# Windowed attention and a gated FFN: transposes of x, q and k moved from TensorE to the DMA engines

## The chip, the cores and the metric

One core of a Trainium2 chip runs the whole kernel. The time is device microseconds of one execution; a median over several executions is quoted.

## The reference

```python
# q, k, v: (4 batches, 8 heads, 768, 64) f32
keep = (pos_k < 4) | ((pos_q - pos_k >= 0) & (pos_q - pos_k < 128))   # 4 sink keys and a window of 128
a = softmax(where(keep, q @ k.T / sqrt(64), -1e9));  attn = a @ v
x = attn.transpose(0, 2, 1, 3).reshape(3072, 512)
xn = x / rms(x) * rms_g
out = (silu(xn @ w_gate) * (xn @ w_val)) @ w_out      # 512 -> 1536 -> 512
```

## The kernel before

The 3072 rows are 24 blocks of 128 rows (six to a batch), and four blocks make a group for the FFN: groups 0 to 5. All matmuls are bf16. TensorE's order is written by hand; a list of attention units ("slots", four to a block) is woven between the FFN's parts. The orders of the other engines come from a scheduler.

Three operands have to be turned so that their columns lie on the partitions: q and k of each block (for the scores) and the normalised x (for the gate and value matmuls). TensorE does it, 128x128 at a time into PSUM, and ScalarE copies the result to SBUF:

```python
MANUAL = {mybir.EngineType.PE}

def unit_t(g):                                   # q and k of block g: 8 transposes, one copy
    b, t = divmod(g, NT)
    if t == 0:
        QKT[b] = qkt.tile([P, 2, HP, S], BF16, name="qkT")
    ps = pp[0].tile([P, 512], FP32, name="pqk", tag="b1").bitcast(BF16)
    transposes(ps, QS.pop(g), 0)
    transposes(ps, KS_.pop(g), HP * P)
    nc.scalar.copy(out=QKT[b]...[:, :, t * P:(t + 1) * P], in_=ps...)

def unit_x(g):                                   # x of block g: 4 transposes, one copy
    ...
    ps = pp[0].tile([P, 512], FP32, name="pxt", tag="b1").bitcast(BF16)
    xr = XR.pop(g)
    for kt in range(KTN):
        nc.tensor.transpose(out=ps[:, kt * P:(kt + 1) * P],
                            in_=xr[:, kt * P:(kt + 1) * P], identity=ident)
    nc.scalar.copy(out=XNT[G][:, :, tb * P:(tb + 1) * P], in_=ps...)

def step(g):                                     # the attention slots of one block (cut)
    ...
    if g - 3 < NB:
        slots[0].append(lambda: unit_x(g - 3))
    if g + 2 < NB:
        slots[2 if t != 5 else 1].append(lambda: unit_t(g + 2))
```

The gate and value matmuls of a group read XNT of all its four blocks. At the second block of a batch, `unit_sink` lets VectorE copy the four sink keys out of the first block's turned k:

```python
def unit_sink(b):
    ...
    nc.vector.tensor_copy(out=ksv[pr, :, hi * NS:(hi + 1) * NS], in_=QKT[b][pr, 1, :, 0:NS])
```

SP (SyncE) issues only the 24 stores of the output, from three buffers that ScalarE fills. All loads are issued by GpSimd and run until 98 us. Group 0's weave, which the change also touches:

```python
n = 9
weave(fb, slots[0:n])                # 12 gate/value parts of half a group, 9 slots
for G in range(NG):                  # for group 0: the 12 output parts, 15 slots
    ...
    weave(parts, slots[n:n1], 1)
```

The softmax here doesn't subtract the row's maximum and nothing guards it: scores larger than these inputs give would overflow.

Of the kernel before, what the change touches and what calls it, by code (L numbers as in the profile page):

```python
# [12 lines left out]
BF16 = mybir.dt.bfloat16  # L13
I32 = mybir.dt.int32

P = 128
# [3 lines left out]
def kernel(  # L20
# [13 lines left out]
    nc = tc.nc  # L34
# [7 lines left out]
    NT = S // P  # L42
    NB = B * NT
    HP = H // 2
    KTN = DM // P
    FTN = DFF // P
    GB = 4
    NG = NB // GB
    GN = GB * P
    VW = D + 1  # L50
    HW = 4 * VW
    KSW = P + 2 * NS
    inv_sqrt_d = 1.0 / math.sqrt(D)
    POOL_MASK_FROM = 2
    MANUAL = {mybir.EngineType.PE}

    const = ctx.enter_context(tc.tile_pool(name="const", bufs=1))
    ld = ctx.enter_context(tc.tile_pool(name="ld", bufs=3 * NT))
# [18 lines left out]
    QS, KS_, V16 = {}, {}, {}  # L77
# [128 lines left out]
    def unit_t1(g, i):  # L206
# [8 lines left out]
            in_=ps[:, 0:HP * P].rearrange("p (x c) -> p x c", c=P),  # L215
        )

    def unit_t(g):
        b, t = divmod(g, NT)
        if t == 0:  # L220
            QKT[b] = qkt.tile([P, 2, HP, S], BF16, name="qkT")
        ps = pp[0].tile([P, 512], FP32, name="pqk", tag="b1").bitcast(BF16)
        transposes(ps, QS.pop(g), 0)
        transposes(ps, KS_.pop(g), HP * P)
        nc.scalar.copy(  # L225
            out=QKT[b].rearrange("p i h s -> p (i h) s")[:, :, t * P:(t + 1) * P],
            in_=ps.rearrange("p (x c) -> p x c", c=P),
        )
# [84 lines left out]
    def unit_av(g, u):  # L313
        b, t = divmod(g, NT)
        pv = pp[0].tile([P, 512], FP32, name="pv", tag="pv", bufs=2)
        if t >= 2:
            nc.tensor.matmul(
                out=pv[:, 0:HW], lhsT=ESK[(b, t)],
                rhs=VSK[b][:, 4 * u:4 * u + 4, :],
                start=True, stop=False, skip_group_check=True,  # L320
            )
        for j in range(2):
            for hi in range(2):
                h = 4 * u + 2 * j + hi
                x = 2 * hi + j
                dest = pv[:, (h - 4 * u) * VW:(h - 4 * u + 1) * VW]
                if t >= 1:
                    nc.tensor.matmul(  # L328
                        out=dest, lhsT=E[(g - 1, u)][:, x, 1, :],
                        rhs=V16[b][:, t - 1, h, :],  # L330
                        start=(t == 1), stop=False, skip_group_check=True,
                    )
                nc.tensor.matmul(  # L333
                    out=dest, lhsT=E[(g, u)][:, x, 0, :], rhs=V16[b][:, t, h, :],
                    start=(t == 0), stop=True, skip_group_check=True,
                )
        E.pop((g - 1, u), None)
        if u == 0:
            X16[g] = xpool.tile([P, H, D], BF16, name="x16")
        pvv = pv[:, 0:HW].rearrange("p (h c) -> p h c", c=VW)  # L340
        rden = small.tile([P, 4], FP32, name="rden")
        nc.vector.reciprocal(out=rden, in_=pvv[:, :, D])  # L342
        nc.vector.tensor_tensor(  # L343
            out=X16[g][:, 4 * u:4 * u + 4, :], in0=pvv[:, :, 0:D],
            in1=rden.unsqueeze(2).to_broadcast((P, 4, D)), op=ALU.mult,
        )
        if u == 0:
            MS[g] = small.tile([P, 2], FP32, name="ms")
        xh = X16[g][:, 4 * u:4 * u + 4, :].rearrange("p h d -> p (h d)")
        sq = xpool.tile([P, DM // 2], BF16, name="sq")  # L350
        nc.scalar.activation(
            out=sq, in_=xh, func=ACT.Square, scale=1.0 / math.sqrt(DM),
            accum_out=MS[g][:, u:u + 1],
        )
        if u == 1:
            x16 = X16.pop(g).rearrange("p h d -> p (h d)")
            ms = MS.pop(g)
            m = small.tile([P, 1], FP32, name="m")
            nc.vector.scalar_tensor_tensor(
                out=m, in0=ms[:, 0:1], scalar=1e-6, in1=ms[:, 1:2],  # L360
                op0=ALU.add, op1=ALU.add,
            )


            y = small.tile([P, 1], FP32, name="y")
            nc.vector.tensor_scalar(
                out=y.bitcast(I32), in0=m.bitcast(I32), scalar1=-0.5,
                scalar2=float(0x5f3759df), op0=ALU.mult, op1=ALU.add,
            )
            r = small.tile([P, 5], FP32, name="r")  # L370
            nc.vector.scalar_tensor_tensor(
                out=r[:, 0:1], in0=y, scalar=y, in1=m, op0=ALU.mult, op1=ALU.mult,
            )
            nc.vector.tensor_scalar(  # L374
                out=r[:, 1:2], in0=r[:, 0:1], scalar1=-5 / 16, scalar2=21 / 16,
                op0=ALU.mult, op1=ALU.add,
            )
            for i, c in ((1, -35 / 16), (2, 35 / 16)):
                nc.vector.tensor_scalar(
                    out=r[:, i + 1:i + 2], in0=r[:, i:i + 1], scalar1=r[:, 0:1],  # L380
                    scalar2=c, op0=ALU.mult, op1=ALU.add,
                )
            nc.vector.tensor_tensor(
                out=r[:, 4:5], in0=r[:, 3:4], in1=y, op=ALU.mult,
            )
            XR[g] = xpool.tile([P, DM], BF16, name="xr")
            nc.vector.scalar_tensor_tensor(
                out=XR[g], in0=x16, scalar=r[:, 4:5], in1=gb,
                op0=ALU.mult, op1=ALU.mult,
            )  # L390

    def unit_x(g):
        G, tb = divmod(g, GB)
        if tb == 0:
            XNT[G] = xtpool.tile([P, KTN, GN], BF16, name="xnt")
        ps = pp[0].tile([P, 512], FP32, name="pxt", tag="b1").bitcast(BF16)
        xr = XR.pop(g)
        for kt in range(KTN):
            nc.tensor.transpose(  # L399
                out=ps[:, kt * P:(kt + 1) * P], in_=xr[:, kt * P:(kt + 1) * P],  # L400
                identity=ident,
            )
        nc.scalar.copy(  # L403
            out=XNT[G][:, :, tb * P:(tb + 1) * P],
            in_=ps[:, 0:KTN * P].rearrange("p (k c) -> p k c", c=P),
        )
# [44 lines left out]
    def parts_o(G, tb):  # L451
        st = {}

        def part(i):
            if i == 0:
                st["po"] = pp[0].tile([P, 512], FP32, name="po", tag="b1")
            for ft in range(4 * i, 4 * i + 4):
                nc.tensor.matmul(  # L458
                    out=st["po"], lhsT=HT[(G, ft // 2)][:, ft % 2, tb * P:(tb + 1) * P],
                    rhs=wo[:, ft, :], start=(ft == 0), stop=(ft == FTN - 1),  # L460
                )
            if 4 * i + 4 == FTN:
                osb = opool.tile([P, DM], FP32, name="osb")

                nc.scalar.mul(osb, st["po"], 0.5)  # L465
                row = (G * GB + tb) * P
                nc.sync.dma_start(out=out[row:row + P, :], in_=osb)

        return [lambda i=i: part(i) for i in range(FTN // 4)]


    def step(g):


        b, t = divmod(g, NT)
        slots = [[], [], [], []]
        if g < NB:
            slots[0].append(lambda: unit_s(g, 0))
            slots[2].append(lambda: unit_s(g, 1))
            if t == 1:  # L480
                slots[1].append(lambda: unit_sink(b))
            if t in (2, 4):
                slots[1].append(lambda: unit_sink_scores(b, t))
        if g <= NB:
            slots[1].append(lambda: unit_av(g - 1, 0))
            slots[3].append(lambda: unit_av(g - 1, 1))
        if g - 3 < NB:
            slots[0].append(lambda: unit_x(g - 3))
        if g + 2 < NB:
            slots[2 if t != 5 else 1].append(lambda: unit_t(g + 2))  # L490
        return slots

    def weave(parts, slots, upto=0, first=False):

        n, i = len(parts) - upto, 0
        for s, f in enumerate(parts):
            if first:
                f()
            while i < len(slots) and i < (s + 1) * len(slots) / n:
                for u in slots[i]:  # L500
                    u()
                i += 1
            if not first:
                f()

    with tc.manual_schedule(engines=MANUAL):
# [18 lines left out]
        )  # L525
        PT_BUFS[0] = 1


        fa, fb = [], []
        for ft in range(0, FTN, 2):  # L530
# [20 lines left out]
            slots += step(g)  # L551
        slots[3].pop()
        slots[7].pop()
        n = 9
        weave(fb, slots[0:n])
        for G in range(NG):
            parts = [] if G == 0 else [
                f for ft in range(FTN) for f in parts_f(G, (ft,), slice(0, GN))
            ]
            for tb in range(GB):  # L560
                parts += parts_o(G, tb)
            n1 = 3 + 4 * ((G + 2) * GB + 2 - 5) + 1
            weave(parts, slots[n:n1], 1)
            n = n1
# [33 lines left out]
```

## Time and profile before

| | |
|---|---|
| time, median of the first 3 runs | 275.36 us (274.61 to 275.64) |
| TensorE busy, of a span of 272.5 us | 249.1 us |
| TensorE busy from group 1's first gate matmul (80.37 us) to the end, of 192.13 us | 186.97 us |
| a 128x512 matmul in a dense stretch, start to start | 216 ns |
| a 128x128 transpose in a dense stretch, start to start | 57 ns |

From the page of the kernel before, busy time by engine, and the slices of TensorE and of the DMA engines (each digit is the busy share in tenths of 6.8 us):

```profile
span 272.5 us, 4924 instructions
PE 249.1 (91%) x1864; PEld 133.4 (49%) x1864; DVE 186.6 (68%) x493; ACT 156.3 (57%) x297; POOL 96.4 (35%) x129
PE   1637978998999999999999999899999999999994
DMA  9999999999999930120000220000130000210012
```

The busy time of the engines by stretch of the kernel before, in us (the x counts instructions; the DMA share of this view sums packets that overlap, so it can exceed 1 and serves only for comparison; PEclk, the granted clock):

```profile
core 0: us, PE busy (x) PEld busy (x) DVE busy (x) ACT busy (x) POOL busy (x), PEclk, DMA share, GB/s
45.00:68.00 23.00, 21.11 (x227) 15.66 (x228) 19.89 (x56) 17.18 (x34) 16.24 (x19) 1.00 2.12 162
...
80.00:107.00 27.00, 27.00 (x208) 13.40 (x207) 25.10 (x65) 17.82 (x36) 11.42 (x14) 1.00 1.41 104
...
120.00:147.00 27.00, 26.93 (x205) 13.49 (x204) 20.84 (x51) 17.52 (x34) 6.12 (x10) 1.00 0.03 11
```

TensorE is busy in all of the stretches after 80 us. Busy alone does not prove that it is the limit, because a pipelined matmul counts as busy for longer than it holds the array. So one looks at starts. In the chain of work that ended last, four 128x512 matmuls take 0.86 us throughout, and in the timeline eight transposes of q and k occupy the array from 149.97 to 150.42 us, although each has a duration of some 220 ns. Chain and timeline of the kernel before (start, length, what):

```profile
144.84 0.86 PE pvl L417 x4
145.70 0.86 PE pg L417 x4
```

```profile
149.97 0.39 PE L201 MATMUL pqk<-ident,qs 128*128 128x128 bf16 x4
150.19 0.39 PE L201 MATMUL pqk<-ident,ks 128*128 128x128 bf16 x4
150.42 1.89 PE L458 MATMUL po<-wo,hT 128*128 128x512 bf16 x8
...
171.50 1.02 PE L417 MATMUL pg<-xnt,wg 128*128 128x512 bf16 x4 [1.46 <-DVE p_2647 L435]
```

0.45 us for eight is 56 to 57 ns each: this is what a transpose costs a dense TensorE.

### The profile page before, as it was taken

The page shows a single profiled execution, that of the slowest core. Times are in us where ns is not written, and L with a number is a line of the kernel's source. Part 1 is how long each engine was busy: PE and PEld are TensorE (multiplying, and loading weights), DVE is VectorE, ACT ScalarE, POOL GpSimd, SP SyncE. Part 2 cuts the span into 40 slices and gives each one's busy share as a digit, 9 for nine tenths or more (in the row PEclk, how much of TensorE's full clock was granted, in tenths as well). Part 3 has the DMA queues.
Part 4 walks back from the last instruction along what each step waited for, and adds up shares of the span by engine and source line. Part 5 has one row for each costly group of instructions (what it writes and reads, how often), then busy time and mean ns, then how long its engine had stood idle before and what let it go on. Part 6 is the DMA issues. An engine that isn't in the chain of part 4 may idle for free.

```text
span 272.5 us, 4924 instructions
## 1 busy us (share of the span) xinstructions
PE 249.1 (91%) x1864; PEld 133.4 (49%) x1864; DVE 186.6 (68%) x493; ACT 156.3 (57%) x297; POOL 96.4 (35%) x129
## 2 busy tenths in 40 slices
PE   1637978998999999999999999899999999999994
PEld 1325766874554544455444454444544454444441
DVE  2591888799788999437798458698337997078710
ACT  2554847769887666557557557558556353333311
POOL 8996369199997601223112001112322000000000
PEclk9999999999999999999999999999999999999998
DMA  9999999999999930120000220000130000210012
GB/s 58 132 175 186 203 160 182 167 155 149 174 199 183 155 14 0 70 88 0 2 1 2 77 77 2 0 2 0 43 113 2 0 2 19 96 41 0 0 68 86
DMA packets 84230, 21.01 MB, mean 77 GB/s; under 512 B 75440, under 2 KB 81072, under 8 KB 84208
## 3 DMA queue, kind: packets, MB, share of 16 engines
q0 software_dynamic: 80752, 14.42, 67.7%
q1 hardware_dynamic: 3456, 6.29, 6.2%
q8 instruction: 14, 0.23, 0.3%
q14 instruction: 8, 0.07, 0.1%
HBM read 28.57 MB, written 6.29 MB: 128 GB/s over the span
## 4 chain that ended last, share of the span: by engine, by line
PE 70%; DVE 8%; DMA 8%; POOL 6%; ACT 5%; issue 1%; POOLq 0%; ACTq 0%; DVEq 0%
PE po L458 22%; PE pg L417 18%; PE pvl L417 18%; DMA ks<-in_k_dram 5%; PE pT L279 4%; DMA wg<-in_moe_w_gate_dram 3%; PE pqk L201 3%; ACT et L286 2%; PE pxt L399 2%; DVE hT L443 2%; POOL ks L90 2%; PE pv L333 1%; ACT qkT L225 1%; POOL qs L90 1%; POOL v_98 L103 1%
## 5 line engine op out<-in xcount | busy, mean ns | idle before, releaser
L417 PE MATMUL pg<-xnt,wg 128*128 128x512 bf16 (+1 forms) x336 | 74.9, 352 | 2.9 <-ACT xnt L403 1.5
L417 PE MATMUL pvl<-xnt,wv 128*128 128x512 bf16 (+1 forms) x336 | 74.1, 349 | 0.0
L458 PE MATMUL po<-wo,hT 128*128 128x512 bf16 x288 | 66.8, 379 | 0.0
L430 ACT ACTIVATE th<-pg 128x512 bf16<-128x512 f32 x72 | 42.8, 595 | 37.8 <-PE pg L417 37.6
L286 ACT ACTIVATE et<-pT 128x1024 bf16<-128x1024 f32 (+1 forms) x48 | 45.2, 946 | 8.9 <-PE pT L279 8.8
L301 POOL TENSOR_SCALAR_AFFINE_SELECT et<-et 128x512 bf16<-128x512 bf16 x20 | 13.2, 660 | 99.6 <-ACT et L286 99.6
L417 PEld LDWEIGHTS <-wg 128*128 128x128 bf16 x336 | 31.3, 99 | 28.1 <-issue 3.1
L417 PEld LDWEIGHTS <-wv 128*128 128x128 bf16 x336 | 31.2, 98 | 25.4 <-issue 0.6
L458 PEld LDWEIGHTS <-hT 128*128 128x128 bf16 x288 | 26.7, 98 | 27.6
L465 ACT ACTIVATE osb<-po 128x512 f32<-128x512 f32 x24 | 14.4, 598 | 24.4 <-PE po L458 19.0
L90 POOL DMA_DIRECT2D ks<-in_k_dram x24 | 21.6, 901 | 6.9 <-DMA wo<-in_moe_w_out_dram 3.5
L225 ACT COPY qkT<-pqk 128x1024 bf16<-128x1024 bf16 x21 | 21.2, 1007 | 5.1 <-PE pqk L201 5.1
L90 POOL DMA_DIRECT2D qs<-in_q_dram x24 | 21.7, 904 | 6.6 <-DMA wo<-in_moe_w_out_dram 2.6
L342 DVE RECIPROCAL rden<-pv 128x4 f32<-128x4 f32 x48 | 8.5, 176 | 19.6 <-PE pv L333 19.5
L279 PE MATMUL pT<-qkT 64*128 64x256 bf16 (+1 forms) x192 | 18.9, 276 | 2.5 <-ACT qkT L225 1.7
L299 DVE TENSOR_TENSOR et<-et,masks 128x1024 bf16<-128x1024 bf16 (+1 forms) x28 | 18.1, 647 | 1.4 <-ACT et L286 1.1
L201 PE MATMUL pqk<-ident,qs 128*128 128x128 bf16 x96 | 10.3, 236 | 7.1 <-DMA qs<-in_q_dram 6.9
L403 ACT COPY xnt<-pxt 128x512 bf16<-128x512 bf16 x24 | 14.0, 581 | 4.6 <-PE pxt L399 4.5
L279 PEld LDWEIGHTS <-qkT 64*128 64x128 bf16 x192 | 6.2, 95 | 18.5 <-issue 17.9
L333 PEld LDWEIGHTS <-et 128*128 128x128 bf16 x192 | 13.5, 100 | 3.2 <-DVE et L299 1.2
L328 PEld LDWEIGHTS <-et 128*128 128x128 bf16 x160 | 12.9, 99 | 3.8 <-DVE x_319 L343 0.7
L399 PE MATMUL pxt<-ident,xr 128*128 128x128 bf16 x96 | 9.9, 229 | 4.2 <-DVE r L374 2.6
(303 smaller groups left out, 341.7 us busy)
## 6 DMA issues: line engine op xcount, KB each, us to landing
out_dram<-osb SPq DMA_DIRECT2D x24, 256.0 KB, 2.0
qs<-in_q_dram POOLq DMA_DIRECT2D x24, 128.0 KB, 7.0
ks<-in_k_dram POOLq DMA_DIRECT2D x24, 128.0 KB, 6.7
wg<-in_moe_w_gate_dram POOLq DMA_DIRECT2D x4, 384.0 KB, 10.0
wv<-in_moe_w_val_dram POOLq DMA_DIRECT2D x4, 384.0 KB, 11.2
wo<-in_moe_w_out_dram POOLq DMA_DIRECT2D x2, 768.0 KB, 11.0
v_98<-in_v_dram POOLq DMA_DIRECT2D x6, 128.0 KB, 7.9
v_100<-in_v_dram POOLq DMA_DIRECT2D x6, 128.0 KB, 7.6
```

Of the source, the lines that this page charges most:

```text
L90: nc.gpsimd.dma_start(out=tl, in_=src[b, :, t * P:(t + 1) * P, :].rearrange("h t d -> t h d"),)
L201: nc.tensor.transpose(out=ps[:, c0 + hp * P:c0 + (hp + 1) * P], in_=src[:, 2 * hp:2 * hp + 2, :], identity=ident,)
L225: nc.scalar.copy(out=QKT[b].rearrange("p i h s -> p (i h) s")[:, :, t * P:(t + 1) * P], in_=ps.rearrange("p (x c) -> p x c", c=P),)
L279: nc.tensor.matmul(out=pT[:, hi, j * 256:j * 256 + w], lhsT=QKT[b][pr, 1, hp, t * P:(t + 1) * P], rhs=QKT[b][pr, 0, hp, t * P:t * P + w], ...
L286: nc.scalar.activation(out=et[:, :, 0:nq, :].rearrange("p x n c -> p x (n c)"), in_=pT.rearrange("p i (j c) -> p (i j) c", c=256)[:, :, 0: ...
L299: nc.vector.tensor_tensor(out=ev, in0=ev, in1=mv, op=ALU.mult)
L333: nc.tensor.matmul(out=dest, lhsT=E[(g, u)][:, x, 0, :], rhs=V16[b][:, t, h, :], start=(t == 0), stop=True, skip_group_check=True,)
L399: nc.tensor.transpose(out=ps[:, kt * P:(kt + 1) * P], in_=xr[:, kt * P:(kt + 1) * P], identity=ident,)
L417: nc.tensor.matmul(out=ps[:, i * n:(i + 1) * n], lhsT=w_sb[:, kt, ft * P:(ft + 1) * P], rhs=XNT[G][:, kt, cols], start=(kt == 0), stop=(kt ...
L430: nc.scalar.activation(out=st["th"], in_=st["pg"], func=ACT.Tanh, scale=0.5)
L458: nc.tensor.matmul(out=st["po"], lhsT=HT[(G, ft // 2)][:, ft % 2, tb * P:(tb + 1) * P], rhs=wo[:, ft, :], start=(ft == 0), stop=(ft == FTN ...
L465: nc.scalar.mul(osb, st["po"], 0.5)
```

## The change

The intent is to take work from the engine that bounds the kernel. x from block 8 on, and q and k of the blocks from 12 on (but not of the first block of a batch), are turned by DMA transposes on SP's queue, straight from SBUF to SBUF. SP now has an order written by hand. The q and k transposes are issued a block earlier than TensorE did them, those of x as soon as x is normalised. The spread of slots in group 0 changes as well.

```diff
-    MANUAL = {mybir.EngineType.PE}
+    MANUAL = {mybir.EngineType.PE, mybir.EngineType.SP}
+    DMA_T_FROM = 12
+    DMA_X_FROM = 8
+    WEAVE_FROM = 9
 ...
+    def by_dma(g):
+        return g >= DMA_T_FROM and g % NT > 0
 ...
     def unit_t(g):
+        if by_dma(g):
+            for i, src in enumerate((QS.pop(g), KS_.pop(g))):
+                nc.sync.dma_start_transpose(
+                    out=QKT[b][:, i, :, t * P:(t + 1) * P],
+                    in_=src.rearrange("p h d -> p (h d)"))
+            return
 ...                                            # in unit_av, once x of block g is normalised
+            if g >= DMA_X_FROM:
+                ...
+                nc.sync.dma_start_transpose(
+                    out=XNT[G][:, :, tb * P:(tb + 1) * P], in_=XR.pop(g))
 ...
     def unit_x(g):
+        if g >= DMA_X_FROM:
+            return
 ...                                            # in step
-        if g + 2 < NB:
+        if g + 2 < NB and not by_dma(g + 2):
             slots[2 if t != 5 else 1].append(lambda: unit_t(g + 2))
+        if g + 3 < NB and by_dma(g + 3):
+            slots[2].append(lambda: unit_t(g + 3))
 ...                                            # group 0: 24 slots over all its 24 parts
-        n = 9
-        weave(fb, slots[0:n])
+        n = 0
         for G in range(NG):
-            parts = [] if G == 0 else [...]
+            parts = fb if G == 0 else []
 ...
```

(`WEAVE_FROM` is larger than the number of groups and does nothing here. The manual schedule is also opened anew after the prologue.)

More of the change, by code (lines that the diff above doesn't have):

```diff
@@ L221, in unit_t @@
             QKT[b] = qkt.tile([P, 2, HP, S], BF16, name="qkT")
+        if by_dma(g):
+            for i, src in enumerate((QS.pop(g), KS_.pop(g))):
+                nc.sync.dma_start_transpose(
+                    out=QKT[b][:, i, :, t * P:(t + 1) * P],
+                    in_=src.rearrange("p h d -> p (h d)"),
+                )
+            return
         ps = pp[0].tile([P, 512], FP32, name="pqk", tag="b1").bitcast(BF16)
@@ L390, in unit_av @@
             )
+            if g >= DMA_X_FROM:
+                G, tb = divmod(g, GB)
+                if tb == 0:
+                    XNT[G] = xtpool.tile([P, KTN, GN], BF16, name="xnt")
+                nc.sync.dma_start_transpose(
+                    out=XNT[G][:, :, tb * P:(tb + 1) * P], in_=XR.pop(g),
+                )
     def unit_x(g):
+        if g >= DMA_X_FROM:
+            return
         G, tb = divmod(g, GB)
@@ L395, in unit_x @@
             XNT[G] = xtpool.tile([P, KTN, GN], BF16, name="xnt")
+        xr = XR.pop(g)
         ps = pp[0].tile([P, 512], FP32, name="pxt", tag="b1").bitcast(BF16)
-        xr = XR.pop(g)
         for kt in range(KTN):
@@ L526 @@
         PT_BUFS[0] = 1
+    with tc.manual_schedule(engines=MANUAL):
         fa, fb = [], []
@@ L553 @@
         slots[7].pop()
-        n = 9
-        weave(fb, slots[0:n])
+        outs = []
+        n = 0
         for G in range(NG):
-            parts = [] if G == 0 else [
-                f for ft in range(FTN) for f in parts_f(G, (ft,), slice(0, GN))
-            ]
-            for tb in range(GB):
-                parts += parts_o(G, tb)
+            parts = fb if G == 0 else []
+            for ft in range(FTN if G > 0 else 0):
+                parts += parts_f(G, (ft,), slice(0, GN))
+                if ft % 3 == 2 and outs:
+                    parts += outs.pop(0)
+            outs = [parts_o(G, tb) for tb in range(GB)]
+            if G < WEAVE_FROM or G == NG - 1:
+                for o in outs:
+                    parts = parts + o
+                outs = []
             n1 = 3 + 4 * ((G + 2) * GB + 2 - 5) + 1
```

## The prediction

> **What bounds the kernel now.** TensorE: 249.1 us busy of 272.5 on the page, and full in every stretch of the table of windows from 68 us on, but for 1.5 us near 165 us. Busy is not peak, so I looked at the starts of matmuls: 128x512 ones come every 216 ns (four in 0.86 us in the chain of waits), and from 80 us to the end the excess over such a steady pace sums to about 3 us. The losses lie earlier: 16 us in the first 25 us, while loads land, 3.5 us at 35:45 and 2 us at 60:70.
>
> **What the change removes.** Four transposes of x for blocks 8 to 23 (64 matmuls) and eight of q and k for blocks 13 to 17 and 19 to 23 (80), with 16 copies by ScalarE of 0.58 us and 10 of 1.01 us. A transpose's duration is 220 to 236 ns, but they are pipelined: in the timeline eight of q and k take the array from 149.97 to 150.42 us, 57 ns each. 144 x 57 ns = 8.2 us of TensorE, all after 80 us, where it is the limit, so nearly all should leave the span. ScalarE (50 to 65% busy there) is off the critical path; its 19 us are worth nothing by themselves.
>
> **What it adds.** 36 DMA transposes of 128 KB on SP's queue, in order with the 24 stores. No trace here has one. The Trainium skill (DMA: Bandwidth & Descriptors, Latency and other measured facts) gives 261 GB/s for a DMA transpose, and VectorE: DVE Perf Modes, The three transpose paths, 1309 ns for 128x128. An estimate from these and the 2.0 us to landing of a 256 KB store here: 2 to 4 us each. The DMA engines are 90% busy until 95 us and nearly idle afterwards, so twelve per group of 40 us fit.
>
> **Is it in time?** The last x of a group decides: it is normalised at 110.0, 151.2, 192.2 and 229.9 us, and the gate matmuls that read it start near 120.4, 160.7, 202 and 238 us: 8 to 10 us for a transpose that needs about 3. The q and k transposes are issued a step (10 us) earlier than before. SP's waits in order hold a store for at most a few us, and three output buffers cover that. I expect no new TensorE wait above 1 us.
>
> **What moves.** In group 0 the slots are spread over gate/value and output parts together, so about 12 slots of attention run beside the former, where 9 did. VectorE is already busy 19.9 of 23 us at 45:68, and attention costs it more than TensorE: 0 to 2 us more here, something of it given back after.
>
> **Predicted.** 275.4 - 8.2 + 0.6 = 267.8 us (-2.8%); 264.8 to 272.0 in 8 of 10. Faster by over 2%: 0.70; within: 0.22; slower: 0.08.
>
> **What would show it.** 144 matmuls fewer; from the first gate matmul of group 1 (80 us) to the end about 8 us less, matmuls still 216 ns apart; transposes land in 2 to 4 us; neither x's nor q/k's appear among TensorE's waits; 45:80 changes by less than 2 us.
>
> **What would make it wrong.** A DMA transpose that occupies the engines for over 3.4 us (twelve would fill a group's 40 us), or lands after over 8 us: TensorE would wait at each group's start. Stores held behind transposes could stall ScalarE's output copies and, through PSUM, TensorE. The reordering of group 0 could cost more than 2 us.

## The result, and the profile after

The changed kernel took 265.88 us (265.62 to 266.04, 4 runs) against 274.99 us (274.11 to 275.64, 4 runs): ratio 0.967, interval 0.9639 to 0.9701.

The page of the changed kernel:

```profile
span 264.3 us, 4691 instructions
PE 241.3 (91%) x1695; PEld 125.9 (48%) x1720; DVE 185.6 (70%) x493; ACT 139.7 (53%) x271; POOL 95.6 (36%) x129
PE   0646998998999999999999999999999999999994
DMA  8999999999999999154103362312330111200022
```

TensorE has 7.8 us less to do (x1720 weight loads against x1864: the 144 transposes; 25 matmul records are missing from this trace, so weight loads are the safer count). ScalarE has 26 instructions and 16.6 us less, and its share was and is far from full. The DMA engines have gained work everywhere after 95 us. Where it came off is seen by cutting both traces at the first gate matmul of group 1. These are the rows of the kernel before and then of the changed one, columns as above:

```profile
80.37:272.50 192.13, 186.97 (x1251) 90.70 (x1247) 128.82 (x317) 102.94 (x201) 33.63 (x49) 1.00 0.27 42
```

```profile
81.34:264.30 182.96, 177.52 (x1085) 82.75 (x1103) 127.23 (x317) 86.73 (x175) 32.25 (x47) 1.00 0.44 69
```

The stretch became 9.2 us shorter and TensorE's busy time in it 9.45 us less; the time in which it is not busy, 5.2 us before, is 5.4 us after. That last pair has to be read with care. Most of the missing records lie in this stretch (1085 matmuls to 1103 weight loads), and they leave 22 holes of some 53 ns, 1.2 us in all, that were not idle: in 21 of them the matmuls on both sides start 430 to 442 ns apart, about twice 216, so that one is missing. So some 8.2 us of the 9.2 are work that went away, and about 1.0 us is a wait that became shorter (1.46 us to 0.43 us, shown below).

The DMA issues of the changed kernel (size where known, median us from issue to landing), and the timeline of SP's queue around 168 us:

```profile
out_dram<-osb SPq DMA_DIRECT2D x24, 256.0 KB, 2.2
xnt<-xr SPq DMA_TRANSPOSE x16, 2.4
qkT<-qs SPq DMA_TRANSPOSE x10, 2.4
qkT<-ks SPq DMA_TRANSPOSE x10, 2.5
```

```profile
167.03 1.19 SPq L409 DMA_TRANSPOSE xnt<-xr  x1
168.31 1.22 SPq L231 DMA_TRANSPOSE qkT<-qs  x1
169.62 1.22 SPq L231 DMA_TRANSPOSE qkT<-ks  x1
```

SP takes 1.2 us to issue one, and it lands 2.4 us after the issue began. While the loads still run it is 7 to 8.8 us (the first six), and the last load lands at 104.4 us in place of 98.3. What TensorE waits for in the changed kernel, longest first (us in total, times, longest; the first four lines, all of the first 45 us). No DMA transpose stands anywhere in the list:

```profile
PE pqk L205 <- DMA qs<-in_q_dram: 5.3, 2, 5.1
PE pxt L422 <- DVE r L388: 2.6, 1, 2.6
PE pxt L422 <- DVE xr L401: 2.0, 2, 1.1
PE pqk L205 <- DMA ks<-in_k_dram: 1.8, 2, 1.1
```

And in its timeline, the gate matmul that had waited 1.46 us before now waits 0.43 us:

```profile
165.98 0.81 PE L440 MATMUL pg<-xnt,wg 128*128 128x512 bf16 x3 [0.43 <-DVE p_2552 L458]
```

### The profile page after: what moved, and what is told of

Same layout as the page of the kernel before. It is cut to its first block, busy times and chain, and to the rows that moved or that the text cites. A ratio compares the mean times of both kernels' runs of the same rounds, so it can differ in the third digit from the quotient of the medians.

```text
span 264.3 us, 4691 instructions
## 1 busy us (share of the span) xinstructions
PE 241.3 (91%) x1695; PEld 125.9 (48%) x1720; DVE 185.6 (70%) x493; ACT 139.7 (53%) x271; POOL 95.6 (36%) x129
## 4 chain that ended last, share of the span: by engine, by line
PE 79%; DVE 9%; ACT 4%; issue 2%; POOL 2%; DMA 2%; POOLq 0%; ACTq 0%; DVEq 0%
PE po L481 24%; PE pg L440 22%; PE pvl L440 21%; PE pT L293 4%; PE pqk L205 2%; DMA qs<-in_q_dram 2%; DVE hT L466 2%; PE pv L347 2%; PE pv L342 1%; ACT et L300 1%; DVE et L313 1%; PE pss L274 1%; PE pv L331 1%; DVE xr L401 1%; ACT sq L365 1%
## 5 line engine op out<-in xcount | busy, mean ns | idle before, releaser
L481 PE MATMUL po<-wo,hT 128*128 128x512 bf16 x278 | 65.7, 379 | 0.5
L315 POOL TENSOR_SCALAR_AFFINE_SELECT et<-et 128x512 bf16<-128x512 bf16 x20 | 13.2, 660 | 89.2 <-ACT et L300 89.2
L342 PEld LDWEIGHTS <-et 128*128 128x128 bf16 x160 | 12.9, 99 | 3.8 <-DVE x_319 L357 0.7
L239 ACT COPY qkT<-pqk 128x1024 bf16<-128x1024 bf16 x11 | 11.1, 1008 | 2.5 <-PE pqk L205 2.5
L205 PE MATMUL pqk<-ident,qs 128*128 128x128 bf16 x56 | 6.6, 252 | 6.0 <-DMA qs<-in_q_dram 5.3
L393 DVE TENSOR_SCALAR r<-r 128x1 f32<-128x1 f32 x48 | 10.2, 212 | 1.0
L320 POOL TENSOR_SCALAR_AFFINE_SELECT et<-et 128x512 bf16<-128x512 bf16 x16 | 10.2, 636 | 0.0
```

The lines of the kernel that those rows point to most:

```text
L205: nc.tensor.transpose(out=ps[:, c0 + hp * P:c0 + (hp + 1) * P], in_=src[:, 2 * hp:2 * hp + 2, :], identity=ident,)
L315: nc.gpsimd.affine_select(out=et[:, :, 0, :], in_=et[:, :, 0, :], compare_op=ALU.is_ge, fill=0.0, base=0, pattern=[[0, 4], [1, P]], channe ...
L342: nc.tensor.matmul(out=dest, lhsT=E[(g - 1, u)][:, x, 1, :], rhs=V16[b][:, t - 1, h, :], start=(t == 1), stop=False, skip_group_check=True,)
L481: nc.tensor.matmul(out=st["po"], lhsT=HT[(G, ft // 2)][:, ft % 2, tb * P:(tb + 1) * P], rhs=wo[:, ft, :], start=(ft == 0), stop=(ft == FTN ...
```

## The experiments

**How to compare runs here.** The edits below are shortened. In the rounds of four of the runs ("after, again", "DMA transposes twice", "more blocks by DMA" and "ScalarE's copies kept, in place") the times fall into two clusters 1.8 us apart: the kernel before took 273.3 to 273.7 or 275.1 to 275.7 us, and the changed kernel 263.7 to 264.1 or 265.7 to 265.9. In the other rounds the kernel before spreads as wide (273.1 to 275.7), with less clear clusters. In the profiled runs of the changed kernel, the second half of group 0 (its first gate matmul) began at 47.18 us in one and 45.13 us in another, and the rest was the same to 0.02 us. The timelines show where the two part. Up to 22.5 us they are 0.2 us apart; then TensorE goes over from half pace to full pace, in one near 30 us and in the other near 25 us. First "after", then "after, again":

```profile
22.64 1.87 PE L440 MATMUL pg<-xnt,wg 128*128 128x256 bf16 x8 [0.67 <-ACT xnt L426]
27.43 1.89 PE L440 MATMUL pvl<-xnt,wv 128*128 128x256 bf16 x8
31.62 1.05 PE L440 MATMUL pvl<-xnt,wv 128*128 128x256 bf16 x8
```

```profile
22.45 1.87 PE L440 MATMUL pg<-xnt,wg 128*128 128x256 bf16 x8 [0.67 <-ACT xnt L426]
26.72 1.05 PE L440 MATMUL pvl<-xnt,wv 128*128 128x256 bf16 x8
29.56 1.05 PE L440 MATMUL pvl<-xnt,wv 128*128 128x256 bf16 x8
```

Why full pace comes later in some executions is not shown. So besides the time, two stretches are given below, which do not depend on this: from the last gate matmul of group 0's first half to group 1's first gate matmul (S0), and from there to the end of the span (S1). They are read from the timelines of the profiled runs.

| run | time us | ratio to before | S0 us | S1 us |
|---|---|---|---|---|
| before | 275.36 | 1 | 38.60 | 192.1 |
| after | 265.88 | 0.967 | 38.14 | 183.0 |
| after, again | 264.87 | 0.9657 | 38.15 | 183.0 |
| TensorE's transposes kept | 274.25 | 1.0004 | 38.14 | 191.7 |
| x only | 270.40 | 0.9853 | 38.13 | 187.6 |
| q and k only | 269.21 | 0.9822 | 38.13 | 187.6 |
| new spread of group 0 only | 273.49 | 0.9979 | 38.35 | 192.2 |
| old spread of group 0 | 265.75 | 0.969 | 38.59 | 183.0 |
| SP's order left to the scheduler | 278.36 | 1.0157 | 38.13 | 195.9 |
| x from block 4 | 264.49 | 0.9666 | 38.70 | 182.8 |
| DMA transposes twice | 264.88 | 0.9648 | 38.27 | 182.8 |
| more blocks by DMA | 270.18 | 0.9848 | 42.29 | 184.2 |
| ScalarE's copies kept | 273.04 | 0.9961 | 40.13 | 183.0 |
| ScalarE's copies kept, in place | 289.53 | 1.0526 | 38.14 | 206.6 |

The theory (A) is the prediction's: the gain is TensorE's own time, 57 ns for each transpose. The rival (B) is that the gain is ScalarE's: its copies, and the PSUM buffers that had to wait for them. A smaller rival (C) puts what exceeds 8.2 us down to the new spread of group 0.

### TensorE's transposes kept

```diff
             for i, src in enumerate(...):               # in unit_t, beside the DMA transposes
+            dead = pp[0].tile([P, 512], FP32, name="pqk", tag="b1").bitcast(BF16)
+            transposes(dead, QS[g], 0);  transposes(dead, KS_[g], HP * P)
         if g >= DMA_X_FROM:                             # in unit_x
+            dead = pp[0].tile(...);  for kt ...: nc.tensor.transpose(out=dead[...], in_=xr[...], ...)
             return
```

> The changed kernel, but TensorE still does the 144 transposes into PSUM banks that nobody reads; the data come by DMA as in the changed kernel, ScalarE copies nothing. Theory A (the gain is TensorE's own time, 144 x 57 ns): the gain is lost again, 274 us (273 to 275.5), ratio to before 0.993 to 1.002. Rival B (the gain is ScalarE's 19 us of copies and the PSUM buffers that waited for them): it stays near 266 us, ratio 0.967.

Measured: 274.25 us, ratio 1.0004 (0.9956 to 1.0053). The row from group 1 on:

```profile
81.42:273.10 191.68, 185.68 (x1227) 90.78 (x1247) 129.08 (x317) 87.25 (x175) 33.37 (x49) 1.00 0.45 67
```

ScalarE has the 87 us of the changed kernel, not the 103 us of the kernel before, and the data come by DMA; only the matmuls are back. S1 is within 0.5 us of the kernel before. So taking 16 us from ScalarE was worth about 0.5 us on balance, and putting TensorE's 144 transposes back costs 8.7 of the 9.1 us gained there. This refutes B as the account of the gain. (The dead transposes take PSUM buffers again, too. But the kernel before had only one TensorE wait of over 0.15 us after 80 us, of 1.46 us, so waits for buffers cannot have been the 8.2 us.)

### ScalarE's copies kept (twice, and both miscarried)

```diff
+            dead = xpool.tile([P, 1024], BF16, name="deadqk")      # 512 for x
+            nc.scalar.copy(out=dead, in_=wg[:, 0, 0:1024])
```

> The changed kernel, with ScalarE doing 26 copies of the old sizes (16 of 512 and 10 of 1024 columns, from a weight tile to scratch) at the old places, TensorE doing no transposes of those blocks. Theory A: no change from the changed kernel, 266 us (265.3 to 267.5), ratio 0.966 to 0.973. Rival B: most of the gain goes, over 270 us.

Measured: 273.04 us, as B would have it. But the profile shows a different reason. S1 is 183.0 us, that of the changed kernel to the hundredth; the loss is all before it. The copies read a weight tile and depend on nothing else, so the scheduler moved all 26 of them ahead, into the first 80 us: there ScalarE was busy 34.07 us of the 35 from 47 to 82 us, and one of them held up ScalarE for 4.4 us until a weight load had landed:

```profile
ACT deadx L418 <- DMA wg<-in_moe_w_gate_dram: 4.4, 1, 4.4
```

The run says nothing about copies at their old places. The second attempt let each copy read the block that had just been turned, at the place of the old copy:

```diff
+            dead = xpool.tile([P, KTN, P], BF16, name="deadx")
+            nc.scalar.copy(out=dead, in_=XNT[G][:, :, tb * P:(tb + 1) * P])   # q, k: from QKT
```

> The run with ScalarE's copies kept, mended: there the copies read a weight tile, waited for nothing and were all scheduled into the first 80 us. Now each copies the block that the DMA engines have just transposed (16 of 512 columns, 10 of 1024) at the place of the old copy. Theory A: ScalarE's time there is off the critical path, 266 us (265 to 267.3), and from the first gate matmul of group 1 to the end 183 us (182.7 to 184). Rival B: over 270 us, that stretch over 187 us.

Measured: 289.53 us, 16 us slower than before. Two of its waits:

```profile
ACT deadqk L247 <- DMA qkT<-ks: 19.4, 10, 3.7
ACT deadx L425 <- DMA xnt<-xr: 17.9, 9, 6.8
```

The scheduler set the copies on ScalarE so early that ScalarE, which works in order, stood 37.3 us waiting for transposes to land, and with it the exponentials and activations behind them. Again not a test of B. It is a lesson for its own sake: the changed kernel is fast because no engine has to stand before a transpose that is still under way. What the old copies alone, with no wait, would cost at their old places was not measured. So it is shown that the gain needs TensorE's transposes gone; that it would be whole with ScalarE still copying is not shown.

### The two parts by themselves

```diff
-    DMA_T_FROM = 12      # x only
+    DMA_T_FROM = NB
```
```diff
-    DMA_X_FROM = 8       # q and k only
+    DMA_X_FROM = NB
```

> Only x (from block 8) goes through the DMA engines; q and k stay on TensorE. Theory A: 64 x 57 ns = 3.6 us of the gain, and with it whatever the reordering of group 0 and of ScalarE gives (0 to 1 us): 271 us (270 to 272), ratio 0.982 to 0.989. If the x transposes' place right before a group's gate matmuls were what mattered, nearly the whole gain would be here: 267 us.

> Only q and k (from block 12) go through the DMA engines; x stays on TensorE. Theory A: 80 x 57 ns = 4.6 us of the gain: 270 us (269 to 271.3), ratio 0.978 to 0.986. The two parts should add up to the whole within 1 us.

Measured: 270.40 us (0.9853) and 269.21 us (0.9822). Rows from group 1 on, x only and then q and k only:

```profile
80.94:268.50 187.56, 182.18 (x1164) 87.23 (x1183) 127.18 (x317) 95.24 (x185) 33.08 (x48) 1.00 0.35 54
```

```profile
80.74:268.30 187.56, 180.85 (x1148) 86.29 (x1167) 128.24 (x317) 93.93 (x191) 32.16 (x47) 1.00 0.37 57
```

Each takes 4.6 us from S1 (192.1 to 187.6), and together they take 9.1: the parts add. For q and k that is just the estimate, 80 x 57 ns = 4.6 us. For x it is 0.9 us over the estimate of 64 x 57 ns = 3.6 us. The difference is the wait near 171 us: 1.46 us before and also with q and k only, 0.48 us with x only, 0.43 us with both.

### Group 0's new spread

The first kernel has the new spread (and SP's order by hand) and no DMA transposes; the second has the DMA transposes and the old spread (`n = 9; weave(fb, slots[0:n])` put back).

```diff
-    DMA_T_FROM = 12
-    DMA_X_FROM = 8
+    DMA_T_FROM = NB
+    DMA_X_FROM = NB
```

> The kernel before with the new spread of group 0 and SP in program order, and no DMA transpose at all. My prediction said that the new spread loses 0 to 2 us, put at 0.6: 275.5 us (274.5 to 277). Rival C (the gain beyond 8.2 us comes from the new spread): 273.5 to 274.5 us, ratio 0.993 to 0.997.

> The changed kernel with the old spread of group 0. As predicted: 265.5 us (264 to 266.3), as fast or faster than the changed kernel's 265.9. Rival C: 266.5 to 267.5 us.

Measured: 273.49 us (0.9979, 0.9917 to 1.0041) and 265.75 us (0.969), neither distinguishable by time. S0 is 38.60 and 38.59 us with the old spread, and with the new one 38.35 without DMA transposes and 38.13 to 38.27 in the eight runs with them that change nothing else in this stretch. The new spread gains 0.3 to 0.5 us; the prediction had it lose 0.6. The traces show where. In the kernel before, the first gate matmul of group 0's second half waits for ScalarE's copy of x, and the transposes of block 6 follow it; with the new spread they come first and fill that wait. The kernel before, then the changed one (again):

```profile
45.61 1.03 PE L417 MATMUL pg<-xnt,wg 128*128 128x256 bf16 x8 [0.79 <-ACT xnt L403]
46.48 0.39 PE L201 MATMUL pqk<-ident,qs 128*128 128x128 bf16 x4
```

```profile
44.33 0.38 PE L205 MATMUL pqk<-ident,qs 128*128 128x128 bf16 x4 [0.18 <-DVE p L458]
45.13 1.05 PE L440 MATMUL pg<-xnt,wg 128*128 128x256 bf16 x8 [0.19 <-DVE hT L466]
```

(For this reason S0 may not start at that gate matmul: the new spread has moved these transposes, 0.45 us, across it.) Rival C had the right sign, and the reading of its small size needed the stretch, not the time.

### SP's order left to the scheduler

```diff
-    MANUAL = {mybir.EngineType.PE, mybir.EngineType.SP}
+    MANUAL = {mybir.EngineType.PE}
```

> The changed kernel with SP's order left to the scheduler, which moves all q and k transposes of a batch ahead of the stores and of most x transposes. Theory A with SP waiting in order: the first three stores wait for the q and k of block 17, which land near 80 us, so ScalarE runs out of output buffers, and later x transposes come behind eight q and k transposes of 1.2 us issue each: waits of TensorE of 2 to 8 us, 268 to 274 us. Rival (the order does not matter, since SP is idle most of the time): 266 us.

Measured: 278.36 us (1.0157), slower than the kernel before. TensorE's longest wait, then ScalarE's timeline at that moment, then SP's waits:

```profile
PE pqk L205 <- ACT osb L488: 10.6, 1, 10.6
```

```profile
93.10 0.60 ACT L488 ACTIVATE osb<-po 128x512 f32<-128x512 f32 x1 [13.05 <-DMA out_dram<-osb]
```

```profile
SPq L231 <- DMA qs<-in_q_dram: 45.9, 4, 42.2
```

The scheduler put ten q and k transposes ahead of the first three stores. SP stood up to 42 us before the loads of q; the stores behind went out only at 86.6 us (in the changed kernel the first three were out by 78.7 us); ScalarE, out of its three output buffers, stood 13 us; and TensorE 10.6 us. The Trainium skill (DMA: Bandwidth & Descriptors, Anatomy of one DMA — SWDGE (gpsimd) path) says that DMA engines do not wait on semaphores and that the wait happens on the issuing sequencer before dispatch; this trace agrees for SP's queue, with its wait of 42 us: one transpose that is not ready holds everything behind it on SP. The mechanism was expected and its size (2 to 8 us) was put too low. The wait was not all: after it the granted clock was 0.50 until about 98 us, and four 128x512 matmuls took 1.91 us in place of 1.03. By an estimate from these, half pace from 93.5 to 98.2 us cost 2.3 us, which with the 10.6 us of the wait makes the 12.9 us by which S1 is longer than the changed kernel's. The order by hand is worth 12 to 13 us, more than the whole gain.

### x from block 4

```diff
-    DMA_X_FROM = 8
+    DMA_X_FROM = 4
```

> x goes through the DMA engines from block 4 on, so during the loads as well. There a transpose took 7 to 8.8 us to land, and block 7 is normalised 4 to 5 us before the gate matmuls of group 1 need it. Theory (lateness at a group's start): 16 x 57 ns = 0.9 us saved, and TensorE waits 3 to 5 us near 81 us: 268.5 us (267 to 270.5). If the latency were hidden there too: 265 us.

Measured: 264.49 us (0.9666, 0.9604 to 0.9729), the same as the changed kernel within the noise. In the timeline the gate matmul of group 1 does wait for an x transpose, but for less than expected:

```profile
79.79 0.38 PE L440 MATMUL pg<-xnt,wg 128*128 128x512 bf16 x1 [1.18 <-DMA xnt<-xr]
```

S0 and S1 together are 221.5 us against 221.1 of the changed kernel. The lateness exists (1.2 us), but most of it is paid for by the 16 transposes saved (0.9 us); the expected 3 to 5 us was wrong.

### The DMA transposes twice

```diff
+                dead = xpool.tile([P, HP, P], BF16, name="dead")
+                nc.sync.dma_start_transpose(out=dead, in_=...)      # before each real one
                 nc.sync.dma_start_transpose(out=..., in_=...)
```

> The changed kernel with every DMA transpose issued twice, the first time into scratch: 72 in place of 36, so 24 per group and some 1.2 us more until each lands. Theory A (the transposes have 7 to 8 us to spare and the DMA engines have room): 266 us (265 to 267.5), no TensorE wait for a DMA transpose. If the DMA engines or SP's issue were near their limit: waits of TensorE at the starts of groups 2 to 5, over 268 us.

Measured: 264.88 us (0.9648) beside 264.87 us (0.9657) of the changed kernel in the same rounds. TensorE waits for no transpose, with 72 of them. The last load landed at 112.7 us in place of 104.0, and some transposes came up to 8.9 us after their issue, but nobody stood before them. So the DMA engines and SP have room for at least twice the transposes; this is why they cost no time here.

### More blocks by DMA

```diff
-        return g >= DMA_T_FROM and g % NT > 0
+        return g >= DMA_T_FROM                       # q, k of blocks 12 and 18 too
+    def x_by_dma(g):
+        return g >= DMA_X_FROM or g in (4, 5, 6)
```

> A version meant to beat both: x of blocks 4, 5 and 6 also goes through the DMA engines (block 7 does not, as it came 1.2 us late at group 1), and q and k of blocks 12 and 18 too. Theory A: another 12 + 16 = 28 transposes, 1.6 us off TensorE: 264.3 us (263.3 to 265.5), of which 0.9 us in the stretch from group 1 on (182.1 us there). If latency under the loads hurts: 266 us or more.

Measured: 270.18 us (0.9848), 5.3 us slower than the changed kernel in the same rounds. VectorE's wait, and TensorE's:

```profile
DVE ksk L253 <- DMA qkT<-ks: 7.2, 2, 5.6
```

```profile
PE pg L443 <- ACT xnt L429: 5.2, 2, 4.5
```

VectorE copies the sink keys out of block 12's turned k. The scheduler had put that copy ahead of work that was ready, the transpose took 7.4 us to land under the loads, and VectorE stood 5.6 us (74.4 to 80.0 us); ScalarE, which waited 5.3 us for VectorE, copied the x of block 7 late, and TensorE stood 4.5 us. This is what the condition `g % NT > 0` of the change avoids. S1 is also 1.2 us longer than the changed kernel's though it has 16 transposes fewer (0.9 us). Most of this is the clock after the stand. The granted clock was 0.50 from 83.1 to 85.0 us and 1.00 from 86 us on, and four matmuls of the same size took 1.87 us and then 1.04:

```profile
83.10 1.87 PE L443 MATMUL pg<-xnt,wg 128*128 128x512 bf16 x4 [4.49 <-ACT xnt L429]
86.64 1.04 PE L443 MATMUL pg<-xnt,wg 128*128 128x512 bf16 x4
```

From 83.10 us, where S1 starts, to 86.64 us it takes 3.54 us; the changed kernel needs 2.60 for the same stretch, with eight transposes more (0.46 us): 1.4 us lost. The remaining 0.7 us was not found out.

### The changed kernel again

> The changed kernel itself, unchanged, on the same chip and in the same rounds as the three others, for comparison with them: 265.9 us (264.3 to 266.3), ratio 0.967; the spread of its runs tells how much the first 47 us differ from run to run.

Measured: 264.87 us (263.68 to 265.9), ratio 0.9657 (0.9615 to 0.9699), with the two clusters described above. Cluster against cluster, the change is worth 9.5 to 9.6 us (273.5 to 263.9, and 275.3 to 265.8). No version tried here was shown to beat it.

## Why the prediction was right

- **What bounds the kernel: right, and shown.** With TensorE's transposes put back and everything else as changed, the gain is gone (274.25 us).
- **144 x 57 ns = 8.2 us: right.** S1 fell by 9.1 us, of which 1.0 us is the wait named below; q and k alone gave the 4.6 us of their estimate. The step that mattered was to cost a transpose by the distance between starts (57 ns), not by its duration of 220 ns, which would have given 32 us, nor by ScalarE's 19 us of copies. The Trainium skill (TensorE: Matmul & The Clock Gate, Part 4: PE-mode transpose) has about 390 ns for one transpose in isolation and about 275 ns in a kernel; the 220 ns here is a duration of that kind and somewhat below it; taken as the cost in a dense stream, a duration is about four times too much.
- **"I expect no new TensorE wait above 1 us": right.** None appears in the changed kernel after 80 us. The DMA transposes landed in 2.4 us, inside the 2 to 4 us predicted. The 7 to 8.8 us under the loads had not been foreseen; the blocks concerned had the time.
- **"0 to 2 us more" in group 0: wrong sign.** It gained 0.3 to 0.5 us. The prediction added up engine times per stretch and took VectorE's larger load in the first part for a loss; it did not see that the moved transposes would fill TensorE's wait of 0.79 us. With 0.6 us expected as a loss, this term was about 1 us off.
- **A term that was missing:** the wait of 1.46 us near 171 us shrank by 1.0 us when x left TensorE. That it goes with x and not with q and k is shown; by which step (the PSUM buffer that x no longer takes, or another order on VectorE) is not. With TensorE's dead transposes, which nobody copied, it was 0.67 us, so most of it went without TensorE's work going: this much of rival B, under 1 us, may be true.
- Sum: 275.4 - 8.2 - 1.0 - 0.5 = 265.7 us, against 265.88 measured and 267.8 predicted. The two terms that were off err the same way, so the hit does not rest on errors that cancel.
- **The rivals that the prediction named** (engines over-occupied, stores held on SP) are real, but not in this kernel: double the transposes cost nothing, and the held stores come at once when SP's order is not written by hand.

## What to carry to other kernels

When one engine is dense, cost what you take from it by the distance between starts in its timeline, and expect just that from the span, whatever else becomes lighter. Moving work to a queue is free only while nobody stands before it: check for every consumer, and for every engine that works in order, when the result lands (here 2.4 us on a quiet DMA, up to 8.8 us beside the loads), and keep what is due first at the front of the issuing queue. Count a long stand of TensorE for more than its length: here, after stands of 4.5 and 10.6 us, it ran at half the clock for 3 to 5 us. To judge effects below the run-to-run spread, cut the traces at a common event that has the same work on both sides in both kernels, and compare stretches. Before calling idle time idle, check for missing records.

## What the Trainium skill lacked or had wrong

- VectorE: DVE Perf Modes, The three transpose paths, and TensorE: Matmul & The Clock Gate, Part 4: PE-mode transpose: they give the duration of a single TensorE transpose (390 ns; about 275 ns in a kernel). What a stream of them costs is missing there (the second page has the spacing of plain matmuls elsewhere, but does not say that it holds for transposes): 57 ns each here, with durations of 220 ns.
- VectorE: DVE Perf Modes, Rules for kernel authors, advises TensorE for a 128x128 transpose if PSUM will do, and does not ask which engine is the limit. Where TensorE is, the opposite paid: 8.2 us of TensorE went away for DMA transposes that cost no time (doubling them: ratio 0.9648 against 0.9657).
- DMA: Bandwidth & Descriptors, Latency and other measured facts: 261 GB/s for DMA transposes, measured on one kernel, without the size of a transfer. By the packet records of this trace the 131 KB of one quiet 128x512 transpose moved in 0.90 us, 146 GB/s, and three in a row were issued 1.3 us apart, 1.2 us of it SP's own issue. The 2.4 us to landing is what a kernel has to plan with.
- DMA: Bandwidth & Descriptors, Issuing engines are not separate DMA queues: it says that DMAs from all issuing engines run on the same 16 engines and interleave, and the slower landing beside the loads agrees, but it has no figure for what that does to latency: a transpose beside the loads (engines 90% busy) took 7 to 8.8 us to land in place of 2.4.
